# Gated MLP behind attention and a soft mixture of experts: another order of token groups and row blocks, and the late weight conversions spread over more turns

## The chip, the cores and the metric

One core of a Trainium2 chip runs the whole program. The metric is device time in microseconds (us), the median over several executions; lower is better. The profile is one further execution, recorded by the hardware profiler. Engines are named as the profile does: PE is TensorE (matmul), DVE is VectorE, ACT is ScalarE, POOL is GpSimd, SP is SyncE, which issues the DMAs here. Each engine works through its own instructions in the order in which the program lists them.

## The reference, cut to what matters

Chunked linear attention gives `x` of 3072 tokens by 512. A soft mixture of 8 experts follows, and then the gated MLP, which is what the change touches:

```python
logits = x @ phi                      # 3072 x 32
d = softmax over tokens; slot_input = d.T @ x
slot_out = experts(slot_input)        # relu MLP, 32 x 512
c = softmax over slots                # 3072 x 32
x = c @ slot_out                      # 3072 x 512
h = x @ w_in                          # 512 x 2048
g = h * sigmoid(1.702 * h)
out = g @ w_out                       # 2048 x 512
```

## The kernel before, in words

Attention and the experts take about 200 us and are not touched. Since `x = c @ slot_out` has rank 32, the kernel never forms it: it multiplies `slot_out` by `w_in` once, which gives `W2s` (32 slots by 2048 columns, held as a high and a low part), and then `h` for a block of columns is one matmul of `W2s` with `cT`, the transposed slot weights.

The MLP runs in 64 turns. A turn is one pair `(tg, f)`: token group `tg` (768 tokens, six tiles of 128; four groups) and row block `f` of `w_out` (128 rows; 16 blocks). `order` lists the pairs. In a turn PE does 18 matmuls of 128x512 (L977, `out_mm`): six token tiles times three products, high by high, high by low and low by high (`ghi`/`whi`, `ghi`/`wlo`, `glo`/`whi`), summed in the six PSUM banks `OB`. In the middle of turn `j`, ahead of its tenth matmul, `do_h(j + 2)` is issued: two matmuls for `h` (L930, into the banks `xt` and `m`), two gates and the high part on ACT (L938, L941), the low part `glo` on DVE (L944). When a group's run of row blocks is broken off, its six sums are copied to SBUF by ACT (`part`, L984); when the group ends later, DVE adds them again (L988).

The weights arrive as 64-bit numbers and must be made 32-bit on the chip. A conversion of 128 x 512 numbers is a load into a staging buffer (`f64`, `NST` of them, L165 on SP), an absolute value on ACT (`cvm`, L174) and four DVE steps (L183, L186, L189, L193). A block of `w_out` is then split by ACT (`whi`, L772) and DVE (`wlo`, L775). 26 conversions are left for the turns of the MLP: `w_out` blocks 2 to 15, and twelve quarters of `w_in` for three column groups `n` = 1, 2, 3 (each serves four row blocks of `w_out`). `turns[j]` lists which conversions are done inside `do_h(j)`; the first three DVE steps stand before `glo`, the fourth after it. A staging buffer is free when step three has read it, and only then SP issues the next load into it.

When the four quarters of a column group of `w_in` are there, `w2_a`, `w2_b` and `w2_c` make its 512 columns of `W2s`. `w2_a` is eight matmuls (profile: x8) into bank `xt`, two ACT copies (L903, L904) and a DVE subtraction (L905). `w2_b` is two matmuls into `xt` again, an ACT copy and a DVE subtraction for the first 128 columns (L888, L889), then an ACT copy of the other columns out of the bank (L912), which waits for that DVE subtraction. `w2_c` splits the rest (L888, L889). In the turns of `w2_b` the `h` matmul for bank `m` is issued first (`at[9]`), and the one for bank `xt` three matmuls later (`at[12]`), because `xt` is still being emptied.

Before the change `order` is group 0 with blocks 0 to 3, group 1 with all 16, group 0 with 4 to 15, then groups 2 and 3. So a new block of `w_out` is wanted each turn from turn 8 to turn 19, and `W2s` columns of group 1, 2, 3 from `do_h(8)`, `do_h(12)`, `do_h(16)`. Seven of the `do_h` (5, 7, 8, 9, 11, 12, 13) hold two conversions.

Of the kernel before, what the change touches and what calls it, by code (L numbers as in the profile page):

```python
# [8 lines left out]
F32 = mybir.dt.float32  # L9
F32R = mybir.dt.float32r  # L10
# [7 lines left out]
def attention_moe_gelu_kernel(  # L18
# [17 lines left out]
    P = 128  # L36
    NHP = H // 2
# [4 lines left out]
    E, DM, F = w1.shape  # L42
    KD = DM // P
    DFF = w_in.shape[1]
    NF = DFF // P
    SE = NS // E
    G = P // NS
    NT = B * S
# [6 lines left out]
    EPS = 1e-9  # L55
    TG = 2 * HS
    HF = 4

    LATE = {1: (2, 3, 4, 5), 2: (5, 6, 7, 8), 3: (9, 11, 12, 13)}
    ROUNDS = 3  # L60
    NST = 4
    F64_MIN = 2.0 ** -15 * 1.125
    CB = 256

# [6 lines left out]
    tailp = tailp_cm.__enter__()  # L71
# [8 lines left out]
    def bank(tag, name):  # L80
        return psp.tile([P, 512], F32, tag=tag, name=name)
# [81 lines left out]
    def load_f64(key, src, pool, n, bufs):  # L163
        t = pool.tile([P, n, 2], U32, tag="f64", name="f64", bufs=bufs)
        SP.dma_start(out=t.rearrange("p n t -> p (n t)"), in_=src)  # L165
        staged[key] = t
# [2 lines left out]

    def convert_abs(key, mask=None):  # L170
        if mask is None:
            mask = ex.tile([P, DM], F32, tag="cvm", name="cvm", bufs=4)
        m = mask
        ACT.activation(out=m, in_=staged[key][:, :, 1].bitcast(F32), func=AF.Abs)  # L174
        magn[key] = m
# [62 lines left out]
    qT, qdT, kT, kd, AT, xT, xn = {}, {}, {}, {}, {}, {}, {}  # L238
# [234 lines left out]
    with tc.manual_schedule():  # L473
# [27 lines left out]
        n = 1  # L501
# [154 lines left out]
        new, old = mr[g % 2], mr[(g + 1) % 2]  # L656
# [114 lines left out]
        def split_hi(f):  # L771
            ACT.activation(out=whi[f], in_=wo[f], func=AF.Copy)  # L772

        def split_lo(f):
            DVE.tensor_tensor(out=wlo[f], in0=wo[f], in1=whi[f].bitcast(F32), op=ALU.subtract)  # L775
# [6 lines left out]
        for e in range(E):  # L782
# [7 lines left out]
            if e == 4:  # L790
# [4 lines left out]
                ex = ex_cm.__enter__()  # L795
# [4 lines left out]

        order = [(0, f) for f in range(HF)] + [(1, f) for f in range(NF)] + [(0, f) for f in range(HF, NF)]
        order += [(tg, f) for tg in range(2, NT // TG) for f in range(NF)]
        first_of = {f: min(order.index((tg, f)) for tg in range(2)) for f in range(NF)}
        w_late = [n for n in range(NE, DFF // 512)]
        turns = {}
        for f in range(2, NF):
            turns.setdefault(first_of[f] - (2 if f < HF else 1), []).append(("out", f))
        for n in w_late:  # L810
            for kk in range(KD):
                turns.setdefault(LATE[n][kk], []).append(("in", n, kk))
        stream = [("out", 1)] + [key for j in sorted(turns) for key in turns[j]]
        ahead_of = iter(stream)

        def load_late():
            key = next(ahead_of, None)
            if key is None:
                return
            if key[0] == "out":  # L820
                src = w_out32[key[1] * P:(key[1] + 1) * P, :]
            else:
                src = w_in32[key[2] * P:(key[2] + 1) * P, key[1] * 1024:(key[1] + 1) * 1024]
            load_f64(key, src, ex, DM, NST)

        for f in range(NST):
            load_late()
# [3 lines left out]
        mp = mp_cm.__enter__()  # L831
# [3 lines left out]
        w2p = w2p_cm.__enter__()  # L835
# [2 lines left out]
        W2s = w2p.tile([P, DFF], F32R, name="W2s")  # L838
        wp = [w2p.tile([P, 512], F32R, name=f"wp{j}") for j in range(2)]
        w2raw = w2p.tile([P, 512], F32, name="w2raw")  # L840
        isumr = w2p.tile([P, P], F32R, name="isumr")
        POOL.tensor_copy(out=isumr, in_=isum4.rearrange("p g s -> p (g s)"))
        for n in w_late:
            w_in_sb[n] = w_in_sb[n - 2] if n > 1 else mp.tile([P, KD, 512], F32, name=f"w_in{n}")
# [42 lines left out]
        def w2_split(bw, o):  # L887
            ACT.activation(out=W2s[:, o], in_=bw, func=AF.Copy)  # L888
            DVE.tensor_tensor(out=W2s[2 * NS:, o], in0=bw[2 * NS:], in1=W2s[2 * NS:, o].bitcast(F32), op=ALU.subtract)  # L889
# [8 lines left out]
        def w2_a(n, tag):  # L898
            bw = bank(tag, "bw")
            for kk in range(KD):  # L900
                PE.matmul(bw[kk * NS:(kk + 1) * NS, :], soT[:, kk, 0, :], w_in_sb[n][:, kk, :],
                          start=True, stop=True, tile_position=(0, kk * NS))
            ACT.activation(out=w2raw, in_=bw, func=AF.Copy)  # L903
            ACT.activation(out=wp[0], in_=w2raw, func=AF.Copy)  # L904
            DVE.tensor_tensor(out=wp[1], in0=w2raw, in1=wp[0].bitcast(F32), op=ALU.subtract)  # L905

        def w2_b(n, tag):
            bw = bank(tag, "bw2")
            for part in range(2):
                PE.matmul(bw, isumr, wp[part], start=(part == 0), stop=(part == 1))  # L910
            w2_split(bw[:, 0:P], slice(n * 512, n * 512 + P))
            ACT.activation(out=w2raw[:, P:], in_=bw[:, P:], func=AF.Copy)  # L912

        def w2_c(n):
            w2_split(w2raw[:, P:], slice(n * 512 + P, (n + 1) * 512))


        NTG = NT // TG
# [5 lines left out]
        def h_mm(j, us=(0, 1)):  # L924
            tg, f = order[j]
            bh.setdefault(j, {})
            for u in us:
                bh[j][u] = bank(HB[u], "bhh")
                t0 = tg % (NTG // 2) * TG + u * HS
                PE.matmul(bh[j][u][:, :HS], W2s[:, f * P:(f + 1) * P], cT[tg // (NTG // 2)][:, t0:t0 + HS], start=True, stop=True)  # L930
            if len(bh[j]) < 2:
                return
            g[j] = mp.tile([P, TG], F32, tag="g", name="g", bufs=2)
            ghi[j] = mp.tile([P, TG], F32R, tag="ghi", name="ghi", bufs=3)
            glo[j] = mp.tile([P, TG], F32R, tag="glo", name="glo", bufs=3)
# [4 lines left out]
        def h_hi(j, o=slice(0, TG)):  # L940
            ACT.activation(out=ghi[j][:, o], in_=g[j][:, o], func=AF.Copy)  # L941
# [4 lines left out]
        def do_h(j):  # L946
            us = (1, 0) if j in bh else (0, 1)
            h_mm(j, [u for u in us if u not in bh.get(j, ())])
            for u in us:
                h_gate(j, u)  # L950
            h_hi(j)
            tg, f = order[j]
            new = first_of[f] == j and f > 1
            if new:
                split_hi(f)
            if j == 1:
                h_lo(j)
                finish_late(0, rest0)
                finish_late(j, convert_late(j))
            else:  # L960
                rest = convert_late(j, ROUNDS if j > 2 else 0)
                h_lo(j)
                if new:
                    split_lo(f)
                finish_late(j, rest)
            abs_late(j + 1)

        ob, part = {}, {}

        def out_mm(j, t, i):  # L970
            tg, f = order[j]
            begin = j == 0 or order[j - 1] != (tg, f - 1)
            end = j == NJ - 1 or order[j + 1] != (tg, f + 1) or (t == NTT - 1 and j == NJ - LAST - 1)
            if begin and i == 0:
                ob[t] = bank(OB[t], "bo")
            a, w = ((ghi, whi), (ghi, wlo), (glo, whi))[i]
            PE.matmul(ob[t], a[j][:, t * P:(t + 1) * P], w[f], start=(begin and i == 0), stop=(end and i == 2))  # L977
            if not end or i < 2:
                return
            r0 = tg * TG + t * P  # L980
            if f < NF - 1:

                part[tg, t] = mp.tile([P, DM], F32, name=f"part{t}")
                ACT.activation(out=part[tg, t], in_=ob[t], func=AF.Copy)  # L984
                return
            o = mp.tile([P, DM], F32, tag="o", name="o", bufs=3)
            if (tg, t) in part:
                DVE.tensor_tensor(out=o, in0=ob[t], in1=part[tg, t], op=ALU.add)  # L988
            elif t % 2 == 0:
                ACT.activation(out=o, in_=ob[t], func=AF.Copy)  # L990
            else:
                DVE.tensor_copy(out=o, in_=ob[t])
            SP.dma_start(out=out[r0:r0 + P, :], in_=o)
# [32 lines left out]
        def w2_rest():  # L1026
# [3 lines left out]


        extra = {(0, 3): w2_rest, (0, 6): lambda: do_h(1), (0, 13): lambda: do_h(2),
                 (5, 4): lambda: w2_a(1, "xt"), (6, 5): lambda: w2_b(1, "xt"), (6, 8): lambda: w2_c(1),
                 (8, 4): lambda: w2_a(2, "xt"), (9, 4): lambda: w2_b(2, "xt"), (9, 8): lambda: w2_c(2),
                 (13, 4): lambda: w2_a(3, "xt"), (14, 2): lambda: w2_b(3, "xt"), (14, 8): lambda: w2_c(3)}

        NJ = NTG * NF
        AHEAD = 2
# [16 lines left out]
        for j in range(NJ - LAST + 1):  # L1055
            at = {n: work for (jj, n), work in extra.items() if jj == j}
            if j > 0:
                at[9] = lambda: ahead(j + AHEAD)
                if j in (6, 9, 14):

                    at[9], at[12] = lambda: h_mm(j + AHEAD, (1,)), at[9]
            do_out(j, at)
# [35 lines left out]
```

## Time and profile before

| what | value |
|---|---|
| median of 3 runs | 513.22 us (511.57 to 513.77) |
| profiled execution, its own time | 512.19 us |
| span of the profile (first to last instruction) | 510.2 us |
| PE busy over the span | 486.4 us (95%) |
| DVE, ACT busy over the span | 272.5 us (53%), 273.6 us (54%) |
| DVE busy in the slices from 204 to 290 us | mostly 9 tenths |
| turns of the MLP | from about 204 us to the end |

The profile counts from the first instruction. "Idle before" in square brackets is how long the engine stood still before a row, with what it waited for. A PE row lasts longer (0.39 us) than the distance to the next (0.23 us), since matmuls overlap.

### The profile page before, as it was taken

The numbers are of one execution on the slowest core, as the hardware profiler recorded it, in microseconds if no ns is written. First come the engines' busy times: TensorE is split into PE (matmuls) and PEld (weight loads), VectorE is DVE, ScalarE is ACT, GpSimd is POOL, SyncE is SP. The second block draws the span as 40 slices with busy tenths as digits, with TensorE's granted clock in tenths as the row PEclk, the third lists the DMA queues.
The fourth block names the chain that finished last, engine by engine and source line by source line (L and its number), as shares of the span: only waits on it lengthen the run. The fifth ranks groups of instructions, "written<-read, shape, count | busy, mean of one in ns | idle before, by whom it ended". The sixth has DMA issues, their size and how long they took to land.

```text
span 510.2 us, 9441 instructions
## 1 busy us (share of the span) xinstructions
PE 486.4 (95%) x3561; PEld 377.9 (74%) x3561; DVE 272.5 (53%) x613; ACT 273.6 (54%) x566; POOL 62.9 (12%) x110
## 2 busy tenths in 40 slices
PE   8999999988999999998989899999999999999997
PEld 5777776876876335776767788888888888888886
DVE  5867967966864113898999853222521222321122
ACT  5777767766754335886766645333444334444332
POOL 4633533532221000000000000000000000000000
PEclk9999999999999999999989999999999999999999
DMA  7899999899899998344435003000300000300003
GB/s 165 212 295 286 263 284 284 249 272 255 225 341 326 358 394 312 120 157 173 166 123 202 6 0 125 0 1 0 125 0 0 1 0 4 122 1 0 1 0 123
DMA packets 82748, 76.18 MB, mean 149 GB/s; under 512 B 54288, under 2 KB 62736, under 8 KB 82704
## 3 DMA queue, kind: packets, MB, share of 16 engines
q1 hardware_dynamic: 82672, 75.58, 47.2%
q8 instruction: 28, 0.46, 0.4%
q14 instruction: 16, 0.13, 0.1%
q0 software_dynamic: 32, 0.00, 0.0%
HBM read 69.28 MB, written 6.29 MB: 148 GB/s over the span
## 4 chain that ended last, share of the span: by engine, by line
PE 67%; DMA 11%; DVE 11%; ACT 4%; issue 3%; SPq 3%; ACTq 0%; DVEq 0%
PE bo L977 42%; DMA k<-in_k_dram 5%; DMA qr<-in_q_dram 5%; PE bhh L930 4%; PE bacc L759 3%; PE bh L737 3%; SPq L124 2%; PE bx L338 2%; PE bx L330 2%; DVE glo L944 2%; PE bs L291 2%; PE bk L255 1%; PE bst L304 1%; PE bt L349 1%; DVE wlo L775 1%
## 5 line engine op out<-in xcount | busy, mean ns | idle before, releaser
L977 PE MATMUL bo<-wlo,ghi 128*128 128x512 f32 x382 | 150.6, 396 | 1.3 <-DVE wlo L775 1.2
L977 PE MATMUL bo<-whi,glo 128*128 128x512 f32 x382 | 150.6, 396 | 0.0
L977 PE MATMUL bo<-whi,ghi 128*128 128x512 f32 x382 | 149.5, 393 | 0.1
L944 DVE TENSOR_TENSOR glo<-g,ghi 128x768 fp32r<-128x768 f32 x64 | 61.2, 956 | 147.5 <-ACT ghi L941 147.5
L938 ACT ACTIVATE g<-bhh 128x384 f32<-128x384 f32 x128 | 56.0, 488 | 126.0 <-PE bhh L930 122.9
L977 PEld LDWEIGHTS bo<-wlo,ghi 128*128 128x128 f32 x382 | 72.1, 189 | 18.7 <-DVE wlo L775 2.6
L977 PEld LDWEIGHTS bo<-whi,glo 128*128 128x128 f32 x382 | 72.0, 188 | 15.7 <-DVE glo L944 0.3
L977 PEld LDWEIGHTS bo<-whi,ghi 128*128 128x128 f32 x382 | 72.2, 189 | 14.3 <-DVE W2s L889 0.5
L941 ACT ACTIVATE ghi<-g 128x768 fp32r<-128x768 f32 (+1 forms) x65 | 54.4, 836 | 2.1
L930 PE MATMUL bhh<-cT,W2s 128*128 128x384 f32 x128 | 33.7, 340 | 4.8 <-DVE W2s L889 2.7
L272 POOL TENSOR_TENSOR qdT<-qT,qtab 128x384 f32<-128x384 f32 x32 | 32.2, 1007 | 45.5 <-PE bx L330 28.3
L294 DVE TENSOR_TENSOR AT<-bs,dec 128x384 f32<-128x384 f32 x64 | 32.5, 549 | 1.4 <-PE bs L291 0.7
L930 PEld LDWEIGHTS bhh<-cT,W2s 128*128 128x128 f32 x128 | 23.9, 188 | 11.5 <-DVE W2s L889 3.5
L291 PEld LDWEIGHTS bs<-qT,kT 64*128 64x128 f32 x384 | 23.9, 187 | 9.5 <-issue 6.3
L291 PE MATMUL bs<-qT,kT 64*128 64x128 f32 x384 | 30.0, 289 | 0.7 <-ACT kT L266 0.7
L263 ACT ACTIVATE qT<-bq 128x384 f32<-128x384 f32 x32 | 22.5, 703 | 13.0 <-PE bq L253 12.9
L244 ACT ACTIVATE q<-qr 128x384 f32<-128x384 f32 x32 | 16.7, 523 | 21.0 <-DMA qr<-in_q_dram 20.8
L338 PE MATMUL bx<-AT,v 128*64 128x128 f32 x384 | 26.6, 273 | 0.0
L279 ACT ACTIVATE kd<-k,dec 128x192 f32<-128x192 f32 x64 | 25.4, 442 | 2.1 <-ACT xn L350 0.7
L255 PE MATMUL bk<-ident,k 128*128 128x128 f32 x96 | 16.4, 281 | 5.5 <-DMA k<-in_k_dram 5.4
L338 PEld LDWEIGHTS bx<-AT,v 128*64 128x64 f32 x384 | 20.6, 137 | 0.1
L330 PE MATMUL bx<-qdT,sa 128*128 128x128 f32 x128 | 19.8, 277 | 0.0
(172 smaller groups left out, 592.5 us busy)
## 6 DMA issues: line engine op xcount, KB each, us to landing
w<-in_moe_w_dram SPq DMA_DIRECT2D x64, 512.0 KB, 5.8
f<-in_moe_w_out_dram SPq DMA_DIRECT2D x15, 512.0 KB, 4.4
qr<-in_q_dram SPq DMA_DIRECT2D x32, 192.0 KB, 4.7
k<-in_k_dram SPq DMA_DIRECT2D x64, 96.0 KB, 3.7
v<-in_v_dram SPq DMA_DIRECT2D x64, 96.0 KB, 3.9
f<-in_moe_w_in_dram SPq DMA_DIRECT2D x12, 512.0 KB, 4.0
out_dram<-o SPq DMA_DIRECT2D x23, 256.0 KB, 2.1
stage<-in_moe_w_in_dram SPq DMA_DIRECT2D x8, 256.0 KB, 4.6
```

Source lines behind the costliest of these rows:

```text
L263: ACT.activation(out=t.rearrange("m (p c) -> m c p", c=R), in_=bq[:, :HS].rearrange("m (c p) -> m c p", c=R), func=AF.Copy)
L272: POOL.tensor_tensor(out=qdT[s], in0=qT[s].rearrange("m (c i) -> m c i", c=R), in1=qtab[:, hp, None, :].to_broadcast([P, R, P]), op=ALU.mult)
L279: ACT.activation(out=t[:, :, h, :], in_=k_t[s][:, :, h, :], func=AF.Copy, scale=dec[:, 2 * hp + h, P - 1:P])
L291: PE.matmul(bs[h][:, cs], kT[s][hs, cs], qT[s][hs, cs], start=True, stop=True)
L294: DVE.tensor_tensor(out=t, in0=bs[h][:, :HS].rearrange("m (c i) -> m c i", c=R), in1=dec[:, 2 * hp + h, None, :].to_broadcast([P, R, P]), ...
L330: PE.matmul(bx[:, c * P:(c + 1) * P], state(s, first + c), qdT[s][:, c, :], start=(c == chunks[0]), stop=False)
L338: PE.matmul(bx[h * D:(h + 1) * D, c * P:(c + 1) * P], v_t[s][:, c, h, :], AT[s, h][:, c, :], start=False, stop=(c == R - 1))
L930: PE.matmul(bh[j][u][:, :HS], W2s[:, f * P:(f + 1) * P], cT[tg // (NTG // 2)][:, t0:t0 + HS], start=True, stop=True)
L938: ACT.activation(out=g[j][:, u * HS:(u + 1) * HS], in_=bh[j][u][:, :HS], func=AF.Gelu_apprx_sigmoid)
L941: ACT.activation(out=ghi[j][:, o], in_=g[j][:, o], func=AF.Copy)
L944: DVE.tensor_tensor(out=glo[j][:, o], in0=g[j][:, o], in1=ghi[j][:, o].bitcast(F32), op=ALU.subtract)
L977: PE.matmul(ob[t], a[j][:, t * P:(t + 1) * P], w[f], start=(begin and i == 0), stop=(end and i == 2))
```

## The change

`NHG = 2` groups now start with blocks 0 to 3 (turns 0 to 7), the third group (`tg` = 2) takes all 16 blocks in turns 8 to 23, then groups 0 and 1 do blocks 4 to 15 (turns 24 to 35 and 36 to 47), and group 3 comes last. A new block of `w_out` is wanted from turn 12 to turn 23. Conversions are placed in `do_h(0)` to `do_h(22)`: `w_in` by `LATE_IN`, `w_out` blocks 4 to 7 by `LATE_OUT`; `split_at` says in which `do_h` a block is split. Three `do_h` (10, 12, 14) hold two conversions. `w2_a` stands in turns 7, 11, 15 and `w2_b`, `w2_c` in 8, 12, 16. Groups 0 and 1 both are broken off, so twelve `part` tiles exist, six with names of their own. To make room, the staging buffers go from 4 to 3 and the `cvm` buffers from 4 to 3, and the constant `isumr` moves to a slot of another pool.

```diff
+    NHG = 2
-    LATE = {1: (2, 3, 4, 5), 2: (5, 6, 7, 8), 3: (9, 11, 12, 13)}
+    LATE_IN = {1: (2, 3, 4, 5), 2: (7, 8, 9, 10), 3: (11, 12, 13, 14)}
+    LATE_OUT = {4: 6, 5: 10, 6: 12, 7: 14}
-    NST = 4
+    NST = 3
...
-            mask = ex.tile([P, DM], F32, tag="cvm", name="cvm", bufs=4)
+            mask = ex.tile([P, DM], F32, tag="cvm", name="cvm", bufs=3)
...
-        order = [(0, f) for f in range(HF)] + [(1, f) for f in range(NF)] + [(0, f) for f in range(HF, NF)]
-        order += [(tg, f) for tg in range(2, NT // TG) for f in range(NF)]
-        first_of = {f: min(order.index((tg, f)) for tg in range(2)) for f in range(NF)}
+        order = [(tg, f) for tg in range(NHG) for f in range(HF)] + [(NHG, f) for f in range(NF)]
+        order += [(tg, f) for tg in range(NHG) for f in range(HF, NF)]
+        order += [(tg, f) for tg in range(NHG + 1, NT // TG) for f in range(NF)]
+        first_of = {f: min(order.index((tg, f)) for tg in range(NHG + 1)) for f in range(NF)}
...
-        turns = {}
+        turns, split_at = {}, {}
         for f in range(2, NF):
-            turns.setdefault(first_of[f] - (2 if f < HF else 1), []).append(("out", f))
+            j = first_of[f] - 2 if f < HF else LATE_OUT.get(f, first_of[f] - 1)
+            turns.setdefault(j, []).append(("out", f))
+            split_at[first_of[f] if f < HF else j + 1] = f
         for n in w_late:
             for kk in range(KD):
-                turns.setdefault(LATE[n][kk], []).append(("in", n, kk))
+                turns.setdefault(LATE_IN[n][kk], []).append(("in", n, kk))
...
-        isumr = w2p.tile([P, P], F32R, name="isumr")
+        isumr = tailp.tile([P, P], F32R, tag="xT", name="isumr", bufs=NHP + 1)
...
-            new = first_of[f] == j and f > 1
+            new = split_at.get(j)
             if new:
-                split_hi(f)
+                split_hi(new)
...
-                    split_lo(f)
+                    split_lo(new)
...
-                part[tg, t] = mp.tile([P, DM], F32, name=f"part{t}")
+                part[tg, t] = mp.tile([P, DM], F32, tag=f"part{t}" if tg in (0, NTG - 1) else f"part{tg}_{t}", name="part")
...
-                 (5, 4): lambda: w2_a(1, "xt"), (6, 5): lambda: w2_b(1, "xt"), (6, 8): lambda: w2_c(1),
-                 (8, 4): lambda: w2_a(2, "xt"), (9, 4): lambda: w2_b(2, "xt"), (9, 8): lambda: w2_c(2),
-                 (13, 4): lambda: w2_a(3, "xt"), (14, 2): lambda: w2_b(3, "xt"), (14, 8): lambda: w2_c(3)}
+                 (7, 4): lambda: w2_a(1, "xt"), (8, 4): lambda: w2_b(1, "xt"), (8, 8): lambda: w2_c(1),
+                 (11, 4): lambda: w2_a(2, "xt"), (12, 4): lambda: w2_b(2, "xt"), (12, 8): lambda: w2_c(2),
+                 (15, 4): lambda: w2_a(3, "xt"), (16, 4): lambda: w2_b(3, "xt"), (16, 8): lambda: w2_c(3)}
...
-                if j in (6, 9, 14):
+                if j in (8, 12, 16):
```

## Rows read from the trace of the kernel before

**Rows 1.** Busy time by stretch; columns as the heading line.

```profile
core 0: us, PE busy (x) PEld busy (x) DVE busy (x) ACT busy (x) POOL busy (x), PEclk, DMA share, GB/s
...
204.00:290.00 86.00, 79.78 (x347) 60.61 (x346) 80.11 (x135) 59.99 (x109) 0.00 (x0) 0.98 0.41 141
290.00:505.00 215.00, 215.00 (x959) 178.46 (x958) 61.04 (x74) 88.05 (x154) 0.00 (x0) 1.00 0.07 26
```

**Rows 2.** Timeline of PE, the `h` pairs of turns 4, 15 and 27.

```profile
226.97 0.52 PE L930 MATMUL bhh<-cT,W2s 128*128 128x384 f32 x2
...
289.63 0.51 PE L930 MATMUL bhh<-cT,W2s 128*128 128x384 f32 x2
...
343.47 0.51 PE L930 MATMUL bhh<-cT,W2s 128*128 128x384 f32 x2
```

**Rows 3.** Timeline of PE, rows with idle time before them.

```profile
220.47 0.50 PE L977 MATMUL bo<-wlo,ghi 128*128 128x512 f32 x1 [1.00 <-DVE wlo L775]
...
239.21 0.44 PE L930 MATMUL bhh<-cT,W2s 128*128 128x384 f32 x1 [1.37 <-DVE W2s L889]
...
257.82 0.44 PE L930 MATMUL bhh<-cT,W2s 128*128 128x384 f32 x1 [2.17 <-ACT w2raw L912]
...
275.16 0.50 PE L977 MATMUL bo<-wlo,ghi 128*128 128x512 f32 x1 [0.22 <-DVE wlo L775]
...
285.02 0.44 PE L930 MATMUL bhh<-cT,W2s 128*128 128x384 f32 x1 [1.29 <-DVE W2s L889]
```

**Rows 4.** Busy time by stretch, around the stops at 239 and 258 us.

```profile
258.60:262.00 3.40, 3.40 (x10) 2.67 (x9) 3.37 (x7) 3.00 (x6) 0.00 (x0) 0.51 0.00 0
...
239.50:255.30 15.80, 15.80 (x74) 11.93 (x73) 14.93 (x26) 11.94 (x22) 0.00 (x0) 1.00 0.42 145
```

**Rows 5.** PE by line, 226.9 to 289.7 us.

```profile
L901 PE MATMUL bw<-w_in,soT 128*32 128x512 f32 x24 | 3.5, 605 | 0.0
L910 PE MATMUL bw<-wp,isumr 128*128 128x512 f32 x6 | 2.0, 412 | 0.0
```

**Rows 6.** Timeline of DVE, 224 to 300 us.

```profile
246.62 0.42 DVE L183 TENSOR_SCALAR wo<-f 128x512 uint32<-128x512 uint32 x1
...
249.70 0.95 DVE L944 TENSOR_TENSOR glo<-g,ghi 128x768 fp32r<-128x768 f32 x1
250.57 0.68 DVE L775 TENSOR_TENSOR wlo<-wo,whi 128x512 fp32r<-128x512 f32 x1
...
252.37 0.68 DVE L905 TENSOR_TENSOR wp<-w2raw,wp 128x512 fp32r<-128x512 f32 x1
...
258.37 0.56 DVE L889 TENSOR_TENSOR W2s<-w2raw,W2s 64x384 fp32r<-64x384 f32 x1 [1.12 <-ACT W2s L888]
...
290.54 0.42 DVE L183 TENSOR_SCALAR wo<-f 128x512 uint32<-128x512 uint32 x1
...
294.40 0.42 DVE L183 TENSOR_SCALAR wo<-f 128x512 uint32<-128x512 uint32 x1
```

**Rows 7.** Timeline of ACT, 224 to 300 us.

```profile
225.34 1.56 ACT L984 ACTIVATE part<-bo 128x512 f32<-128x512 f32 x3
227.35 0.87 ACT L938 ACTIVATE g<-bhh 128x384 f32<-128x384 f32 x2 [0.44 <-PE bhh L930]
228.26 0.85 ACT L941 ACTIVATE ghi<-g 128x768 fp32r<-128x768 f32 x1
...
231.70 0.58 ACT L903 ACTIVATE w2raw<-bw 128x512 f32<-128x512 f32 x1
...
234.75 1.23 ACT L174 ACTIVATE cvm<-f 128x512 f32<-128x512 f32 x2
...
257.28 0.49 ACT L912 ACTIVATE w2raw<-bw 128x384 f32<-128x384 f32 x1 [2.84 <-DVE W2s L889]
```

**Rows 8.** Timelines of SP and of ACT: a load, and who waits for it.

```profile
249.24 0.33 SPq L165 DMA_DIRECT2D f<-in_moe_w_in_dram  x1
...
253.60 0.69 ACT L174 ACTIVATE cvm<-f 128x512 f32<-128x512 f32 x1 [0.51 <-DMA f<-in_moe_w_in_dram]
```

## The prediction

> **What bounds the kernel now.** I read the busy time by stretch first. From 290 us to 505 us PE is busy for all of its 215 us [rows 1]: nothing that the change does to other engines can shorten that part, and the number of matmuls stays the same. From 204 to 290 us PE lacks some 6 us, while DVE is busy for 80 of 86 us [rows 1]. So the prize lies in the first 19 turns, and DVE is the engine to watch.
>
> How large the prize is, I count in two ways. A dense turn is (343.47 - 289.63) / 12 = 4.49 us [rows 2]; with 18 matmuls at 0.23 us that leaves 0.35 us for its `h` pair. From turn 4 to turn 15 the trace needs 289.63 - 226.97 = 62.66 us [rows 2] for eleven turns, which dense would be 49.4 us. Of the 13.3 us over, the matmuls of `w2_a` and `w2_b` are 3.5 + 2.0 = 5.5 us [rows 5], and they stay. That leaves 7.8 us lost. The second count goes by the stops: 1.37 + 2.17 + 0.22 + 1.29 = 5.05 us of idle time [rows 3], the overlap that each of the four stops breaks (0.39 - 0.23 = 0.16 us each, 0.6 us together), and the stretch after the longest stop, 3.40 us at a granted clock of 0.51, the lower of the two levels [rows 4], which gives away half of itself, 1.7 us. Together 7.4 us. The two counts agree within 0.4 us; I take 7.8 us, because the first leaves nothing out.
>
> Then the timeline shows what each stop waited for [rows 3]. Three of the four are an `h` matmul behind the making of `W2s`: either its first 128 columns were late (DVE L889), or bank `xt` had not been emptied (ACT L912). Both come from DVE's queue: L912 itself waited 2.84 us for DVE [rows 7], because L889 stood behind conversions. The fourth is a late `wlo`. A fifth, 1.00 us in turn 3 [rows 3], lies ahead of the stretch.
>
> Why DVE is late is a sum per turn. With two conversions, `glo` and `wlo` DVE needs 252.37 - 246.62 = 5.75 us; with one it needs 294.40 - 290.54 = 3.86 us [rows 6]. A turn has 4.49 us. Every turn with two conversions puts DVE 1.26 us further behind, one with a single conversion gives 0.63 us back, and `do_h(7)` to `do_h(13)` hold six of the seven doubles.
>
> **The change part by part.**
>
> *Removed.* The late `wlo` and the wait for the first columns of `W2s` go: `w2_b` now stands in turn 8 and its columns are wanted in turn 10, `w2_b` in 12 and 16 serves turns 14 and 18. The four stops and the half-clock stretch of the old turns 6 to 14 therefore come off: -7.8 us. The stop in turn 3 stays, since `do_h(0)` to `do_h(4)` are as before.
>
> *What stays late.* In turns 8, 12 and 16 the `h` matmul for bank `xt` (13th place) still waits for L912, thus for L889 on DVE and for ACT. I work out each of the three hand-overs.
>
> Turn 8, by ACT's queue. Turn 7 now is the last of group 1's first run, so its six `part` copies meet `w2_a`. From the end of `w2_a` ACT has in order: L903 and L904 (0.58 us each, 1.2), five `part` copies (three take 1.56 us, so 2.5), two gates 0.87, `ghi` 0.85, two absolute values 1.23, L888 and then DVE's L889 for 128 columns (at most 0.56, the row for 384 columns; I take 0.3 each), L912 0.5 [rows 6, 7]. Sum 7.75 us. PE in that time has 14 matmuls of turn 7, 12 of turn 8, an `h` pair, one single `h` and `w2_b`: 26 x 0.23 + 0.35 + 0.17 + 0.46 = 7.0 us. So a new stop of 0.8 us, with the broken overlap 1.0 us. With L888 and L889 at nothing it would be 0.4, with both at the full 0.56 us it would be 1.5.
>
> Turn 12, by DVE's queue. After turn 8's stop DVE has the rest of the split (0.56), which starts about 0.55 us after PE has resumed because ACT's half comes first; then `do_h(10)` with two conversions and no `wlo` (5.75 - 0.60 = 5.15, the 0.60 being the distance from `wlo` to the next row), `do_h(11)` 3.86, `do_h(12)` 5.15, `wp` 0.60, `do_h(13)` 3.86, L889 0.3, L912 0.5 [rows 6, 7]: 20.5 us. PE does four turns, one `w2_a` and one `w2_b` in 17.95 + 1.17 + 0.5 = 19.6 us [rows 2, 5]. A stop of 0.9 us, about 1.0 with the overlap; between 0.2 and 1.8 if the 20.5 us are 4% off either way.
>
> Turn 16 the same way, with only one double (`do_h(14)`): 0.55 + 0.56 + 5.15 + 3.86 + 3.86 + 0.60 + 3.86 + 0.8 = 19.2 us against 19.6 us. No stop, with 0.4 us to spare.
>
> *Added.* Six `part` copies are 3.1 us of ACT, priced above. They could also hold up group 2: bank 3 is wanted at the tenth matmul of turn 8, 23 x 0.23 + 0.35 + 0.46 = 6.1 us after `w2_a`, and its copy is the third in the queue, done after 1.2 + 1.5 + 0.87 + 0.85 + 1.23 = 5.65 us. Free, but by 0.45 us only; if it slips, the slip is part of the same stop. Six more additions fall on DVE in turn 47, where it is busy for 61 of 215 us [rows 1]: free. A matmul is neither added nor removed.
>
> *Fewer buffers.* A load takes from its issue at 249.24 to 253.60 us, 4.4 us, and already then ACT waited 0.51 us for it [rows 8]. With three buffers the load for the third conversion ahead starts when DVE has done step three of the present one, about one turn before ACT wants it in the stretch with doubles. ACT will stand for up to 1.6 us before some absolute values there. This is hidden behind ACT's next wait, that of the gates for PE (0.44 us in rows 7 and more where ACT has less to do), and behind the first three DVE steps ahead of `glo`. Price 0; if loads took 6.5 us, it would come through at about 1 us per double turn, 3 us in all. Nothing is queued behind a waiting load on SP except the next load: the first output leaves in turn 23, after the last conversion. Moving `isumr` costs nothing: it is one POOL instruction, and POOL has no work after 204 us [rows 1].
>
> *Sum.* -7.8 + 1.0 + 1.0 = -5.8 us. The profiled execution took 512.19 us, so 506.4 us; it lay 1.03 us under the median of the runs, 513.22 us. On the scale of the median the forecast is 507.4 us (-1.1%); with both ends of the two stops it runs from 506.0 to 508.7 us. A change of 0.5%, 2.6 us, is about what a measurement of this kernel can tell from none.
>
> *The clock.* After the stop of 2.17 us the clock was at 0.51, after the one of 1.37 us it stayed at 1.00 [rows 3, 4]. The new stops are shorter than both, so I charge nothing for it. The Trainium skill (TensorE: Matmul & The Clock Gate, Part 1: The HAM clock gate) says that throttled is the default state and activity is what releases it. By that rule a new stop puts the clock at stake just as an old one did, and the sum would be 1.7 us higher for each that trips it. The trace agrees on two levels; it has no row for a stop of 1 us that tripped it.
>
> **Rivals.**
> 1. *No stop is left.* If ACT and DVE rows are a little shorter than taken (the 0.5 and 0.3 us bounds above are near zero), the whole 7.8 us comes back: 505.4 us. For it: both new stops are differences of two sums of 7 and 20 us. Against: both sums err on the same side.
> 2. *The stops are short, but the clock falls after both.* 507.4 + 2 x 1.7 = 510.8 us; after one, 509.1. Against it: the two stops of 1.3 us that did no such thing.
> 3. *The waits only move.* If the three hand-overs cost what the old ones did, only the 0.4 us for the late `wlo` is gone: 512.8 us. For it: L912 still hangs on DVE in all three turns. Against it: DVE had six doubles in seven `do_h` and now has three in five, between singles.
> 4. *Slower: bank `xt` late in all three turns as in the old turn 9.* There the hand-over cost 2.17 + 0.16 + 1.7 = 4.0 us. Three of them are 12.1 us against 7.8 us removed: 517.5 us. It decides from 2.6 us per hand-over on. That needs ACT or DVE to be late by 1.6 us more than worked out in turns 8 and 12 and by 3 us more in turn 16, as with loads of well over 6 us behind three buffers.
>
> **How the numbers follow.** Forecast of two short stops: 0.45. Rival 1: 0.20. Rival 2: 0.13. Rival 3: 0.13. Rival 4: 0.09. Faster by over 0.5% means under 510.65 us: forecast, rival 1 and most of rival 2, 0.77. Within 0.5%: the rest of rival 2 and rival 3, 0.14. Slower: 0.09. The range from 505.0 to 510.6 us holds the forecast with its bounds, rival 1 and most of rival 2, and leaves out rivals 3 and 4.
>
> **What the profile after would show.** PE: no idle time at the old turns 6, 9 and 14; the stop in turn 3 as before; one stop of about 1 us each in turns 8 and 12, both an `h` matmul released by L912, none in turn 16; granted clock 1.00 between. DVE: single conversions of 2.4 us up to turn 7 with idle time between them, busy without a break only from turn 8 to 16. ACT: a solid block from `w2_a` in turn 7 to L912 in turn 8, and waits for DMA before some absolute values. PE dense from turn 17 to the end. The prediction is wrong if a stop above 2 us remains, if the low clock appears again, or if PE stops at the change of groups for a `part` copy.

## The result and the profile after

The changed kernel took 505.11 us (median of 4 runs, 503.24 to 507.97) against 513.15 us before (median of 4 runs; 513.22 with the three known beforehand); the ratio is 0.986 with a 95% interval of 0.983 to 0.990. A later set of six runs beside another sample of the kernel before (e8) gave 506.85 us and 0.988 (0.984 to 0.992). The forecast was 507.4 us, range 505.0 to 510.6 us. One execution of the kernel before that stands beside e1 to e4 took 913.62 us at a mean granted clock of 0.546; the ratios leave it out.

The profiled execution took 504.52 us, with a span of 502.5 us. Because the first 203 us scatter (last section), I compare the MLP by itself: from its first 128x512 matmul to the end of the span. Before it is 510.2 - 204.16 = 306.04 us, after it is 502.5 - 203.01 = 299.49 us, so 6.55 us less.

Busy time by stretch of the changed kernel, for the same lengths as [rows 1] from where its MLP starts:

```profile
core 0: us, PE busy (x) PEld busy (x) DVE busy (x) ACT busy (x) POOL busy (x), PEclk, DMA share, GB/s
203.00:289.00 86.00, 83.62 (x375) 64.84 (x374) 75.17 (x123) 62.17 (x114) 0.00 (x0) 1.00 0.38 134
289.00:502.00 213.00, 210.36 (x943) 174.77 (x941) 70.36 (x90) 87.07 (x153) 0.00 (x0) 1.00 0.10 35
```

PE is busy for 83.6 of 86 us in place of 79.8, DVE for 75 us in place of 80, and the granted clock is 1.00 throughout. The tail of the second stretch is the end of the kernel, after PE's last matmul.

Timeline of PE in the changed kernel: the start of the MLP, the `h` pairs of turns 4, 15 and 17, and every row with idle time before it from turn 1 on. These answer to [rows 2, 3]; line numbers are higher by 2 to 5.

```profile
203.01 1.52 PE L982 MATMUL bo<-whi,ghi 128*128 128x512 f32 x5
...
219.32 0.50 PE L982 MATMUL bo<-wlo,ghi 128*128 128x512 f32 x1 [1.00 <-DVE wlo L777]
...
225.81 0.52 PE L935 MATMUL bhh<-cT,W2s 128*128 128x384 f32 x2
...
246.93 0.44 PE L935 MATMUL bhh<-cT,W2s 128*128 128x384 f32 x1 [0.38 <-ACT w2raw L917]
...
267.68 0.45 PE L935 MATMUL bhh<-cT,W2s 128*128 128x384 f32 x1 [0.82 <-ACT w2raw L917]
...
281.57 0.51 PE L935 MATMUL bhh<-cT,W2s 128*128 128x384 f32 x2
...
291.02 0.51 PE L935 MATMUL bhh<-cT,W2s 128*128 128x384 f32 x2
```

Five stops became three. The one in turn 3 is as before; one stands in turn 8 and one in turn 12, both behind L917 (L912 before), the copy that empties bank `xt`. Turn 16 has none.

Timeline of ACT from turn 7 to the hand-over in turn 8:

```profile
238.15 0.60 ACT L989 ACTIVATE part<-bo 128x512 f32<-128x512 f32 x1 [0.62 <-PE bo L982]
239.40 0.60 ACT L908 ACTIVATE w2raw<-bw 128x512 f32<-128x512 f32 x1 [0.65 <-PE bw L906]
240.03 0.63 ACT L909 ACTIVATE wp<-w2raw 128x512 fp32r<-128x512 f32 x1
240.57 1.07 ACT L989 ACTIVATE part<-bo 128x512 f32<-128x512 f32 x2
241.52 0.87 ACT L943 ACTIVATE g<-bhh 128x384 f32<-128x384 f32 x2
242.43 0.85 ACT L946 ACTIVATE ghi<-g 128x768 fp32r<-128x768 f32 x1
243.18 1.22 ACT L176 ACTIVATE cvm<-f 128x512 f32<-128x512 f32 x2
244.30 1.56 ACT L989 ACTIVATE part<-bo 128x512 f32<-128x512 f32 x3
245.73 0.29 ACT L893 ACTIVATE W2s<-bw 128x128 fp32r<-128x128 f32 x1
246.38 0.49 ACT L917 ACTIVATE w2raw<-bw 128x384 f32<-128x384 f32 x1 [0.36 <-DVE W2s L894]
```

From L908 on this is one block without a gap except the 0.36 us for DVE's L894. It holds what the prediction listed, but three of the five `part` copies come behind the absolute values. It ends at 246.87 us, and PE goes on at 246.93.

Timeline of DVE around the two hand-overs: L894 is the split that L917 waits for (L889 before).

```profile
246.06 0.29 DVE L894 TENSOR_TENSOR W2s<-bw,W2s 64x128 fp32r<-64x128 f32 x1 [1.19 <-ACT W2s L893]
247.46 0.56 DVE L894 TENSOR_TENSOR W2s<-w2raw,W2s 64x384 fp32r<-64x384 f32 x1 [1.11 <-ACT W2s L893]
248.05 0.43 DVE L185 TENSOR_SCALAR wo<-f 128x512 uint32<-128x512 uint32 x1
...
265.49 0.69 DVE L777 TENSOR_TENSOR wlo<-wo,whi 128x512 fp32r<-128x512 f32 x1
266.09 0.68 DVE L195 SCALAR_TENSOR_TENSOR w_in<-cvm,w_in 128x512 f32<-128x512 f32 x1
266.81 0.29 DVE L894 TENSOR_TENSOR W2s<-bw,W2s 64x128 fp32r<-64x128 f32 x1
```

In turn 8 DVE stood idle for 1.19 us before its split: it waited for ACT there. In turn 12 the split came with no idle time before it, at the end of a queue that had run since 247.46 us. Two stops that look alike in the list of waits thus have different owners.

### The profile page after: what moved, and what is told of

Same layout as the page of the kernel before. It is cut to its first block, busy times and chain, and to the rows that moved or that the text cites. A ratio compares the mean times of both kernels' runs of the same rounds, so it can differ in the third digit from the quotient of the medians.

```text
span 502.5 us, 9444 instructions
## 1 busy us (share of the span) xinstructions
PE 483.4 (96%) x3561; PEld 376.9 (75%) x3561; DVE 276.3 (55%) x616; ACT 274.7 (55%) x569; POOL 62.8 (12%) x110
## 4 chain that ended last, share of the span: by engine, by line
PE 84%; DMA 5%; DVE 4%; ACT 3%; SPq 2%; issue 1%; POOL 0%; ACTq 0%; DVEq 0%
PE bo L982 49%; DMA k<-in_k_dram 5%; PE bhh L935 4%; PE bs L293 4%; PE bx L340 3%; PE bacc L761 3%; PE bx L332 3%; PE bh L739 3%; PE bst L306 2%; PE bk L257 2%; PE bq L255 2%; PE bt L351 2%; SPq L126 1%; PE bl L361 1%; DMA f<-in_moe_w_in_dram 1%
## 5 line engine op out<-in xcount | busy, mean ns | idle before, releaser
L176 ACT ACTIVATE cvm<-f 128x512 f32<-128x512 f32 x27 | 17.8, 667 | 9.0 <-DMA f<-in_moe_w_in_dram 7.9
```

## The experiments

MLP time is that of the profiled execution, worked out as above: before 306.04 us, after 299.49 us.

| run | MLP us | median us | ratio to before (95%) |
|---|---|---|---|
| e1, old order, three buffers of each kind | 312.73 | 519.64 | 1.012 (1.009 to 1.015) |
| e7, old order, three `cvm` buffers | 306.54 | 513.33 | 1.002 (0.999 to 1.004) |
| e2, new order, old pace | 314.39 | 520.61 | 1.015 (1.011 to 1.019) |
| e5, old order, conversions placed anew | 306.03 | 511.94 | 1.000 (0.997 to 1.002) |
| e6, no `part` copies of group 1 | 298.31 | 504.55 | 0.984 (0.979 to 0.988) |
| e3, `w2` of group 1 one turn earlier | 297.85 | 505.11 | 0.984 (0.981 to 0.987) |
| e4, planned without stops | 296.57 | 503.89 | 0.981 (0.978 to 0.983) |
| e8, the changed kernel again | 299.57 | 506.85 | 0.988 (0.984 to 0.992) |
| e9, e3 and no conversion before `wlo` of block 3 | 296.53 | 503.93 | 0.981 (0.978 to 0.985) |

**What carries the gain.** The theory: PE lost time to DVE's and the loads' lateness, and spreading the conversions over more turns removes it; the new order is what makes the turns available. Rivals: the later deadlines alone, or better placement alone.

e1 takes only the buffers away from the kernel before:

```diff
-    NST = 4
+    NST = 3
-            mask = ex.tile([P, DM], F32, tag="cvm", name="cvm", bufs=4)
+            mask = ex.tile([P, DM], F32, tag="cvm", name="cvm", bufs=3)
```

> The kernel before with 3 staging buffers and 3 cvm buffers, nothing else changed. Theory (fewer buffers are only free because the conversions are spread): with two conversions in seven of the turns, the second load of a pair starts only when the pair before has been read, some 4.4 us before it is wanted, so ACT and then PE wait: 4 to 8 us slower than before, 517 to 521 us, with absolute values waiting for DMA for over 1 us in the turns with two conversions. Rival (the load is hidden anyway): 513 us, no more DMA waits than before.

It is 6.4 us slower than the kernel before by the medians, as expected. The waits of ACT from 204 to 300 us (total, times, longest), in e1:

```profile
ACT cvm L174 <- DMA f<-in_moe_w_in_dram: 24.1, 8, 5.0
ACT w2raw L912 <- DVE W2s L889: 4.9, 3, 2.6
```

in the kernel before:

```profile
ACT cvm L174 <- DMA f<-in_moe_w_in_dram: 2.0, 2, 1.4
```

and two of the nine PE stops of e1:

```profile
244.68 0.45 PE L930 MATMUL bhh<-cT,W2s 128*128 128x384 f32 x1 [3.62 <-DVE W2s L889]
...
280.55 0.82 PE L930 MATMUL bhh<-cT,W2s 128*128 128x384 f32 x2 [1.41 <-ACT g L938]
```

ACT stands for 24.1 us in eight waits for loads, and behind it stand the gates that PE needs. The rival, that the load is hidden anyway, is out.

e7 takes only the `cvm` buffer away (the second edit of e1):

> The kernel before with 3 cvm buffers and still 4 staging buffers. Theory (it is the staging buffers whose loss costs 6.4 us, as the waits for DMA say): 513 us, no change. Rival (the cvm buffers, which ACT has to wait for until DVE's fourth step): 515 us or more.

It is no slower than the kernel before within the interval, though ACT waits for DVE to free `cvm` buffers. So the `cvm` buffer alone does not make the 6.4 us of e1; the staging buffer is needed for it. Three staging buffers with four `cvm` buffers were not run.

e2 is the changed kernel with the old placement:

```diff
-    LATE_IN = {1: (2, 3, 4, 5), 2: (7, 8, 9, 10), 3: (11, 12, 13, 14)}
-    LATE_OUT = {4: 6, 5: 10, 6: 12, 7: 14}
+    LATE_IN = {1: (2, 3, 4, 5), 2: (5, 6, 7, 8), 3: (9, 11, 12, 13)}
+    LATE_OUT = {f: f + 3 for f in range(4, 16)}
```

> The changed kernel with the new order of groups, but the conversions placed as in the kernel before (seven double turns, the last in turn 18). Theory (the gain is that DVE and the loads are given more turns; later deadlines alone do not free bank xt, which still waits for DVE): stops of 2 us and more behind the hand-over of bank xt come back, 511 to 517 us. Rival (the later deadlines of w_out and W2s alone give the gain): 505 us, no stop over 1 us.

520.61 us: above the expected 511 to 517, so the direction of the theory held and its size was too small. Waits of e2 from 204 to 310 us:

```profile
ACT cvm L176 <- DMA f<-in_moe_w_in_dram: 21.8, 8, 4.6
PEld bhh L935 <- ACT w2raw L908: 10.1, 2, 5.3
PE bhh L935 <- ACT w2raw L908: 9.2, 2, 4.9
```

PE lost 9.2 us in two stops behind L908, in turns 7 and 11. L908 is the copy of `w2_a`, and it stood in ACT's queue behind an absolute value that waited for its load. Behind both stops the granted clock fell as well (0.50 from 247.30 to 251.00 us, 0.60 from 274.8 to 278.0 us). ACT at the first stop:

```profile
245.66 0.66 ACT L176 ACTIVATE cvm<-f 128x512 f32<-128x512 f32 x1 [3.38 <-DMA f<-in_moe_w_in_dram]
246.22 0.59 ACT L989 ACTIVATE part<-bo 128x512 f32<-128x512 f32 x1
246.70 0.60 ACT L908 ACTIVATE w2raw<-bw 128x512 f32<-128x512 f32 x1
```

I had looked at DVE and L917; it was the load, ACT and L908. With the later deadlines but the old pace, and with three buffers of each kind, the kernel is 15 us slower than the changed one. e2 does not say what the later deadlines give with four buffers: its waits are for loads, as in e1, and the new order with four buffers was not run.

e5 leaves the old order and its four buffers, and places the conversions anew:

```diff
-    LATE = {1: (2, 3, 4, 5), 2: (5, 6, 7, 8), 3: (9, 11, 12, 13)}
+    LATE = {1: (4, 4, 4, 5), 2: (6, 6, 7, 8), 3: (9, 10, 11, 13)}
```

> The kernel before (old order, 4 buffers) with its conversions placed anew inside the same turns: LATE = {1: (4, 4, 4, 5), 2: (6, 6, 7, 8), 3: (9, 10, 11, 13)}, so that no conversion stands before the wlo of block 3 and the doubles begin earlier. Theory (the old order gives DVE too few turns, so placement can only shift the stops): 511 to 513.5 us, at most the stop in turn 3 gained. Rival (placement alone is the gain and the new order is not needed): 506 to 508 us.

The stop in turn 3 went, and a longer one came at turn 9. PE's longest stop in e5, and the stretch after it:

```profile
258.71 0.69 PE L930 MATMUL bhh<-cT,W2s 128*128 128x384 f32 x1 [3.62 <-ACT w2raw L912]
```

```profile
258.70:265.00 6.30, 6.29 (x16) 5.04 (x17) 5.72 (x11) 3.22 (x6) 0.00 (x0) 0.55 0.26 64
```

The MLP time is unchanged (306.03 us). This one placement does not prove that no other would do; it shows that this move of doubles inside the old order moved the stops and did not remove them.

**Who owns the two new stops.** e6 leaves out the six `part` copies of group 1, so its sums over blocks 0 to 3 are missing from the output:

```diff
             if f < NF - 1:
+                if tg == 1:
+                    return
```

> The changed kernel without the six part copies of group 1: its sums over blocks 0 to 3 are left out of the output, and its last turn copies in place of adding. Theory (the stop in turn 8 is ACT's queue, 2.5 us of it part copies): ACT reaches L917 some 2.5 us sooner, the stop of 0.38 us in turn 8 goes, and the one of 0.82 us in turn 12, counted from there, shrinks to 0.3 us or less; 0.8 to 1.2 us less MLP time. Rival (bank xt waits for DVE in both turns): both stops stay.

In e6 ACT waits for PE at the place where it was late in the changed kernel, the idle time in turn 8 is gone, and that in turn 12 is 0.28 us in place of 0.82. ACT and then PE in e6:

```profile
245.16 0.28 ACT L893 ACTIVATE W2s<-bw 128x128 fp32r<-128x128 f32 x1 [0.76 <-PE bw L915]
245.80 0.49 ACT L917 ACTIVATE w2raw<-bw 128x384 f32<-128x384 f32 x1 [0.36 <-DVE W2s L894]
```

```profile
267.10 0.45 PE L935 MATMUL bhh<-cT,W2s 128*128 128x384 f32 x1 [0.28 <-ACT w2raw L917]
```

The MLP is 1.2 us shorter. The `part` copies own the stop in turn 8, and the stop in turn 12 is counted from there: from the end of L917 in turn 8 to PE's return in turn 12 it is 267.68 - 246.87 = 20.81 us in the changed kernel and 267.10 - 246.29 = 20.81 us in e6. DVE's queue kept its length and only began 1.16 us earlier, counted from the start of the MLP.

e3 keeps all work and moves `w2` of column group 1:

```diff
-                 (7, 4): lambda: w2_a(1, "xt"), (8, 4): lambda: w2_b(1, "xt"), (8, 8): lambda: w2_c(1),
+                 (6, 4): lambda: w2_a(1, "xt"), (7, 4): lambda: w2_b(1, "xt"), (7, 8): lambda: w2_c(1),
-                if j in (8, 12, 16):
+                if j in (7, 12, 16):
```

> The changed kernel with w2_a, w2_b, w2_c of column group 1 one turn earlier (6, 7, 7 in place of 7, 8, 8), so that its ACT work comes before the six part copies and before the double turn 10. Theory (the stop in turn 8 is ACT's queue, with the part copies in it, and the one in turn 12 is DVE's queue counted from there): the stop in turn 8 (0.38 us idle) goes and the one in turn 12 (0.82 us) shrinks or goes, 1.0 to 1.6 us faster than the changed kernel. Rival (the hand-over itself takes that long wherever it stands): the stop moves to turn 7 and the time stays at 505 us.

From turn 4 on PE has no idle time left. Busy time by stretch in e3:

```profile
222.00:300.00 78.00, 78.00 (x356) 61.82 (x355) 70.16 (x115) 56.83 (x104) 0.00 (x0) 1.00 0.41 133
```

The MLP is 1.64 us shorter than in the changed kernel; the expected 1.0 to 1.6 us holds within 0.1 us, and no stop moved to turn 7, as the rival had it. The median is the same 505.11 us as in the first set of the changed kernel. The first stage scatters by more than 1.6 us (in the profiled execution of e3 the MLP began at 205.05 us, 2.0 us later), and without the trace the experiment would have looked like no change.

**A version without stops.** e4 places everything by the two queues, as its expectation says; e9 reaches the same with e3 and one edit more:

```diff
-    LATE_IN = {1: (2, 3, 4, 5), 2: (7, 8, 9, 10), 3: (11, 12, 13, 14)}
+    LATE_IN = {1: (3, 4, 5, 6), 2: (7, 8, 9, 10), 3: (11, 12, 13, 14)}
```

> The changed kernel with LATE_IN 1: (3, 3, 4, 7), 2: (6, 7, 8, 9), 3: (11, 12, 13, 15), LATE_OUT {4: 6, 5: 10, 6: 11, 7: 14} and w2 of group 1 one turn later (8, 9, 9). do_h(2) holds no conversion any more, so the wlo of block 3 comes 2.4 us earlier. Theory (all that PE still loses after turn 1 are the stops in turns 3, 8 and 12, each a sum over one queue): all three go, 2.5 to 2.8 us faster than the changed kernel, 502.4 us, PE without idle time from turn 3 on. Rival (something else holds part of it, such as the loads behind three buffers): a new stop of about 1 us where two loads follow each other, 503.5 to 505 us.

> The changed kernel with w2 of group 1 one turn earlier (6, 7, 7) and LATE_IN 1: (3, 4, 5, 6), which takes the conversion out of do_h(2). Theory: the stops in turns 3, 8 and 12 all go as in the version planned without stops, by two edits only; 2.7 us less MLP time than the changed kernel, 502 to 503 us. Rival: block 4's conversion shares do_h(6) with the last quarter of group 1, and w2_a waits for it: a stop of 0.5 us or more in turn 6.

Both have no PE stop with idle time from turn 1 on. Busy time of e9:

```profile
210.00:300.00 90.00, 89.89 (x407) 71.36 (x407) 82.45 (x135) 65.20 (x119) 0.00 (x0) 1.00 0.43 134
300.00:495.00 195.00, 195.00 (x870) 161.92 (x869) 56.68 (x68) 77.75 (x137) 0.00 (x0) 1.00 0.08 28
```

The MLP time is 2.9 and 3.0 us below that of the changed kernel, a little more than the 2.7 expected. The stops' own sum says 1.16 + 0.54 + 0.98 = 2.7 us (idle time and 0.16 us of overlap each). The medians, 503.89 and 503.93 us, lie above the expected 502.4 and 502 to 503 us, and that of e4 in the range of its rival. But the stop that the rival wants is not there; in the profile of e4 the MLP began at 205.63 us, 2.6 us later than in that of the changed kernel. e9 beats both kernels: on the same chip its six runs lie between 502.44 and 504.89 us, those of the changed kernel between 505.30 and 510.22.

> The changed kernel unchanged, beside the version planned without stops on the same chip, for the scatter of the first 203 us and for the clock. If the low clock comes only with stops, its granted clock varies (one of four runs had 0.993) and that of the version without stops stays at 0.999 to 1.000. Median 505 us.

e8 repeats the changed kernel on that chip. Its MLP is 299.57 us against 299.49 in the first profile, with the same stops. Its median was 506.85 us, expected 505. The granted clock over the span was between 0.996 and 1.000, that of e9 between 0.997 and 1.000 and not the expected 0.999 to 1.000: the two overlap, so these runs don't show that the short stops cost clock. They don't rule it out either. Of the ten executions of the changed kernel in both sets, the four at 0.993 to 0.997 took 508.2 us on average and the six at 0.999 or more 505.5 us. Both profiles are of the second kind, so where the clock fell in the four is not known; in the 40 executions of the kernel before that stand beside the experiments, without that of 913.62 us, the same split gives 513.1 and 512.8 us.

## Why the prediction was right

- **Removed, -7.8 us.** Right in its mechanism. All four stops of the old turns 6 to 14 and the low clock are gone. The MLP gained 6.55 us with 1.5 us of new stops, so about 8.1 us came off. The term was 0.3 us too small, and e9, which has no stops, shows where. Its `h` pairs of turns 4 and 17:

```profile
225.40 0.52 PE L935 MATMUL bhh<-cT,W2s 128*128 128x384 f32 x2
...
288.94 0.51 PE L935 MATMUL bhh<-cT,W2s 128*128 128x384 f32 x2
```

  These 63.54 us are 5.2 us more than 13 dense turns (58.3 us), so three `w2_a` and three `w2_b` cost 5.2 us. The prediction took off their busy time, 5.5 us, in which a `w2_b` counts 0.67 us; in turn 8 it counts the same two matmuls at 0.46 us. With 5.2 us the loss is 13.3 - 5.2 = 8.1 us.
- **Turn 8.** ACT's queue from the end of `w2_a` (239.33) to the end of L917 (246.87) took 7.54 us, worked out as 7.75; PE's path, without the stop, took 7.06 us, worked out as 7.0. The stop was 0.38 + 0.16 = 0.54 us, forecast 1.0. A difference of two sums of 7 us is good to a few tenths, no better.
- **Turn 12.** From PE's return in turn 8 the queue took 267.62 - 246.93 = 20.7 us (20.5 worked out), PE 19.8 us (19.6). Stop 0.98 us, forecast 1.0.
- **Turn 16.** No stop, as forecast: L917 ended 19.47 us after PE's return in turn 12 (19.2 worked out) and PE came for the bank after 19.73 us (19.6), so 0.26 us were to spare. No stop for a `part` copy at the change of groups either. DVE, forecast busy without a break from turn 8 to 16, stood idle only before the splits until 302.15 us, in turn 19.
- **Fewer buffers, price 0.** Right for this placement. In the changed kernel ACT waited 9.0 us for loads in eight waits, the longest 1.8 us (up to 1.6 forecast). The waits from 204 to 300 us:

```profile
ACT cvm L176 <- DMA f<-in_moe_w_in_dram: 7.9, 6, 1.8
...
ACT cvm L176 <- DMA f<-in_moe_w_out_dram: 1.1, 2, 0.6
```

  No stop of PE hung on them. But the condition was named wrongly: not slower loads would have made the cut dear, but doubles in consecutive turns, and then it costs 6.4 us (e1). The loads of e1 were no slower: from 204 to 300 us their median was 4.0 us for `w_in` and 3.3 us for `w_out`, as in the kernel before.
- **Sum.** -5.8 us forecast, -6.55 us in the MLP; the smaller stop in turn 8 makes 0.46 us of the difference, the larger loss 0.3 us. The median fell by 8.0 us in the first set and by 7.0 in the second; in the profiled execution 1.15 us of the gain is a first stage that happened to be shorter, which the change does not touch. That 505.11 us lies only 0.1 us inside the lower end of the range is in part such chance and not the mechanism; how much, the executions without a profile don't show.
- **Rivals.** No stop left (505.4 us) did not happen in the changed kernel, though its median came near; e9 is that case. The low clock after a short stop did not show in either profile of the changed kernel; for the four executions at a mean clock of 0.993 to 0.997 (under e8) it stays open. That the waits only move is what e5 did in the old order. The slower rival has its likeness in e2, by another owner: the loads.

## What to carry to other kernels

Work out each engine's queue from the last point at which it had idle time to the instruction that hands over a buffer, and set it against the path of the engine that waits; here that gave stops of a microsecond within 0.5 us, and told which edit would remove them (e3, e9). What a buffer taken away costs hung here on the pace of the work, not on its amount: three buffers of each kind were free with single conversions between the doubles (new order) and cost 6.4 us with doubles in a row (old order). Where an early stage scatters by more than the effect, compare the stage that was changed by its own length in the traces.

## What the runs showed of the hardware that I had not expected

- **The untouched first stage scatters by 3 us.** In the eleven profiles the MLP's first 128x512 matmul came between 203.01 and 206.07 us, though nothing before it was changed but the addresses and the number of early loads. The same kernel began its MLP at 203.01 us in one profile and at 205.23 us in the other (e8). In this stage PE waits for loads of `k`, 3.2 to 5.7 us in the profiles; that these waits make the scatter is not shown. The MLP itself repeated within 0.1 us (299.49 and 299.57).
- **Whether the low clock was a loss of its own is open.** After the stop of 2.17 us in the kernel before, 3.4 us ran at the lower level [rows 4], which I booked as 1.7 us. In e7, with the same order, the clock stayed at 1.00, behind stops of 1.89 and 1.68 us too, and after them PE stopped for `wlo` twice:

```profile
269.73 0.50 PE L977 MATMUL bo<-wlo,ghi 128*128 128x512 f32 x1 [0.52 <-DVE wlo L775]
...
275.48 0.51 PE L977 MATMUL bo<-wlo,ghi 128*128 128x512 f32 x1 [0.93 <-DVE wlo L775]
```

  Its MLP took 306.54 us against 306.04. Two readings fit. Either DVE was the bound there, and the time that PE gave away at the low clock was time in which DVE caught up. Or the low clock did cost its 1.7 us, and e7 paid as much for its missing `cvm` buffer: its PE stops from turn 1 on add up to 7.66 us of idle time, those of the kernel before to 6.05 us. No run separates the two.
